# Moving late row loads, reciprocal sums and layer-norm scales of a two-layer attention and gated-MLP kernel to GpSimd

## The chip, the cores and the metric

The kernel runs on one NeuronCore of a Trainium2 chip. The metric is the device time of one execution in microseconds (us). "Before" and "changed" are always timed on the same chip, in the same rounds. In the lines of the profile PE is TensorE (matmuls), PEld its weight loads, DVE is VectorE, ACT is ScalarE, POOL is GpSimd and SP is SyncE, which here only issues transfers. L691 is line 691 of the kernel that is profiled; the same statement has another number in each version.

## The reference

A linear attention layer A and a gated MLP layer B, each behind a layer norm, each applied twice with the same weights, on 2048 rows of 512 numbers in bfloat16:

```python
phi_k = concat([softmax(k @ w_phi), softmax(-(k @ w_phi))])    # 32 heads of 16 features, so sums over 16
kv = einsum("bhsf,bhsd->bhfd", phi_k, v);  z = phi_k.sum(rows)
o  = (phi_q @ kv) / (phi_q @ z + 1e-6)                          # phi_q as phi_k
A(x) = o @ wo
B(x) = (relu(x @ W_gate) * (x @ W_up)) @ W_down
x = x + A(layernorm(x));  x = x + B(layernorm(x));  # and both once more
```

## The kernel before

The program is written as a list of operations with guessed durations (`ii`: how long the engine is held, `lat`: when the result is there). A scheduler walks through them in simulated time, with recorded priorities (`RANKS`), and so fixes the order of instructions on each engine; semaphores are then placed.

The rows are worked on in 16 tiles of 128 rows. For each tile of the first layer: statistics on VectorE, their scale by Ln and Exp on ACT, the normalised tile y on VectorE or GpSimd, its transpose by a DMA from SyncE, key and value matmuls, and then the softmax of the keys:

```python
# ln(l, ts), cut: the scale of one or two tiles
op("act", lambda e: e.activation(lnv[:, a:b, :], mv[:, a:b, 1:2], ACT.Ln, bias=eps[:]), ..., ii=186, lat=295)
op("act", lambda e: e.activation(rstd[:, a:b, :], lnv[:, a:b, :], ACT.Exp, scale=-0.5), ..., ii=94, lat=203)
...
# kv_tile(l, t), cut: exp(+-k), sums over 16 features, their reciprocals, normalised features
for s in range(2):
    op("act", lambda e, s=s: e.activation(ft.ap()[:, s, :], kt.ap(), ACT.Exp, scale=(1.0, -1.0)[s]), ...)
op("dve", lambda e: e.tensor_reduce(zt..., ft..., AX.X, ALU.add), ..., ii=1105, name=f"Z{l}.{t}")
if (l, t) in ACT_RZ:                     # all 16 tiles of the first layer
    op("act", lambda e: e.activation(zt.ap(), zt.ap(), ACT.Ln), ..., ii=150)
    op("act", lambda e: e.activation(rt.ap(), zt.ap(), ACT.Exp, scale=-1.0), ..., ii=150)
else:
    op("dve", lambda e: e.reciprocal(rt.ap(), zt.ap()), ..., ii=420)
op("dve", lambda e: e.tensor_tensor(ft..., ft..., rt... .to_broadcast([P, 32, 16, 2]), ALU.mult), ..., name=f"norm{l}.{t}")
...
# loads: rows 8 to 15 are issued by SyncE, late, between the transposes of y
for t in range(8, 16, 4):
    load_x("sp", t, t + 4)
```

The sums over all tiles of key features times values ("kv sums", L716) need the normalised features of every tile, so TensorE must have VectorE's last tile before the first attention layer can go on.

The softmax here doesn't subtract the row's maximum and nothing guards it: scores larger than these inputs give would overflow.

## Time and profile before

The median was 394.14 us (392.99 to 395.31).

| what | us | view |
|---|---|---|
| span of the profiled run | 392.4 | head of the page |
| TensorE busy | 377.8 (96%) | page, part 1 |
| VectorE, ACT, GpSimd busy | 298.3, 195.4, 42.0 | page, part 1 |
| TensorE waiting for others, all waits of 0.2 us and more | 9.1 (the prediction says 9.5) | waits of TensorE |

Head of the page of the kernel before, and the busy tenths in 40 equal slices of the span (one slice is 9.8 us):

```profile
span 392.4 us, 6587 instructions
...
PE 377.8 (96%) x2413; PEld 212.8 (54%) x2455; DVE 298.3 (76%) x641; ACT 195.4 (50%) x606; POOL 42.0 (11%) x117
...
PE   7889999999999999999999999999999999999996
...
DVE  8799979999897769647678996989998648623424
...
POOL 2006003211211000000000000233102110000000
PEclk9999999999999999999999999999999999999999
```

TensorE is nearly always busy, from the first slice to the last, at a full granted clock. Only a wait of TensorE that goes away can shorten this kernel. This is the table of waits of TensorE in the kernel before: who waited for whom, us in total, times, longest:

```profile
PE pb L586 <- DMA yT<-in_A_wqkv_dram: 1.9, 2, 1.1
PE pb L652 <- DMA yT<-y: 1.7, 2, 1.4
...
PE pb L681 <- DMA wv<-in_A_wqkv_dram: 0.8, 1, 0.8
...
```

The 1.9 us are the transposed loads of the query weights, 1.4 of the 1.7 us a wait for the transposes of y at 24.9 us. The timeline of SyncE's queue (start, duration, engine, line) shows what stands in front of those transposes:

```profile
19.43 0.58 SPq L515 DMA_DIRECT2D x_sb<-in_A_x_dram  x1
20.05 5.50 SPq L634 DMA_TRANSPOSE yT<-y  x3
```

The load of rows 8 to 11 goes out at 19.43 us, the transposes follow. In the chain of waits of the page this transfer is given 4.78 us, where the median of 55 transposes is 2.5 us.

### The profile page before, as it was taken

How to read it: one execution, taken by the hardware profiler on the slowest of the kernel's cores; microseconds unless marked ns; L12 is line 12 of the kernel's file. 1: busy time of each engine (PE TensorE's matmuls, PEld its weight loads, DVE VectorE, ACT ScalarE, POOL GpSimd, SP SyncE). 2: the span in 40 equal slices, each digit the busy share in tenths (PEclk: the TensorE clock that was granted, in tenths of full speed). 3: DMA queues.
4: the chain of work that ended last, by engine and by line, in shares of the span. 5: the costliest groups of instructions: out<-in, count | busy, mean ns of one | idle time of the engine just before them, and what ended most of it. 6: DMA issues, size and time to landing. Idle time of an engine off the chain costs nothing.

```text
span 392.4 us, 6587 instructions
## 1 busy us (share of the span) xinstructions
PE 377.8 (96%) x2413; PEld 212.8 (54%) x2455; DVE 298.3 (76%) x641; ACT 195.4 (50%) x606; POOL 42.0 (11%) x117
## 2 busy tenths in 40 slices
PE   7889999999999999999999999999999999999996
PEld 6434574767655544444444457477865544544443
DVE  8799979999897769647678996989998648623424
ACT  5889969637444235334334574875634333113120
POOL 2006003211211000000000000233102110000000
PEclk9999999999999999999999999999999999999999
DMA  8464492243213221200202000014522221210102
GB/s 217 59 157 70 119 339 81 43 69 67 55 28 80 55 42 27 41 1 13 42 0 42 15 13 2 8 35 69 79 57 55 54 55 40 49 47 0 43 0 67
DMA packets 63008, 22.89 MB, mean 58 GB/s; under 512 B 53920, under 2 KB 62976, under 8 KB 62976
## 3 DMA queue, kind: packets, MB, share of 16 engines
q1 hardware_dynamic: 60144, 20.40, 24.2%
q10 hardware_dynamic: 2832, 2.08, 1.7%
q8 instruction: 19, 0.31, 0.3%
q14 instruction: 13, 0.11, 0.1%
HBM read 7.91 MB, written 2.10 MB: 26 GB/s over the span
## 4 chain that ended last, share of the span: by engine, by line
PE 78%; DVE 10%; DMA 4%; ACT 3%; SPq 2%; issue 1%; POOL 0%
PE pb L842 34%; PE pb L896 17%; PE pb L812 6%; PE pb L681 4%; PE pb L716 4%; PE pb L652 3%; PE pb L749 3%; PE pb L696 3%; PE pb L870 3%; DMA yT<-y 2%; PE pb L898 2%; DVE t L786 2%; DVE z L664 1%; ACT expq L700 1%; DVE stats L600 1%; DMA yT<-in_A_wqkv_dram 1%
## 5 line engine op out<-in xcount | busy, mean ns | idle before, releaser
L850 DVE TENSOR_TENSOR hT<-gate,pb 128x512 bf16<-128x512 bf16 (+1 forms) x100 | 57.4, 576 | 40.6 <-PE pb L842 35.9
L849 ACT ACTIVATE gate<-pb 128x512 bf16<-128x512 f32 (+1 forms) x100 | 50.9, 509 | 69.3 <-PE pb L842 68.7
L842 PE MATMUL pb<-yT,Wu 128*128 128x512 bf16 (+1 forms) x392 | 83.1, 336 | 0.3
L842 PE MATMUL pb<-yT,Wg 128*128 128x512 bf16 (+1 forms) x396 | 81.5, 336 | 0.3
L896 PE MATMUL pb<-Wd,hT 128*128 128x512 bf16 (+2 forms) x322 | 76.0, 372 | 0.3
L842 PEld LDWEIGHTS pb<-yT,Wg 128*128 128x128 bf16 x400 | 38.5, 98 | 29.2 <-DVE x_sb L815 0.2
L842 PEld LDWEIGHTS pb<-yT,Wu 128*128 128x128 bf16 x400 | 38.5, 98 | 28.7
L896 PEld LDWEIGHTS pb<-Wd,hT 128*128 128x128 bf16 x330 | 31.6, 98 | 35.1 <-ACT gate L849 0.3
L664 DVE TENSOR_REDUCE z<-phik 128x64 f32<-128x1024 bf16 x32 | 38.3, 1208 | 8.0 <-ACT phik L663 7.8
L600 DVE BATCH_NORM_STATS2 stats<-x_sb 128x6 f32<-128x512 bf16 x64 | 43.4, 686 | 0.5 <-DMA x_sb<-in_A_x_dram 0.2
L700 ACT ACTIVATE expq<-pb 128x512 bf16<-128x512 f32 x64 | 36.1, 610 | 13.8 <-PE pb L696 13.8
L663 ACT ACTIVATE phik<-pb 128x512 bf16<-128x512 f32 x64 | 35.6, 611 | 11.8 <-PE pb L652 11.8
L786 DVE TENSOR_TENSOR t<-pb,sm 128x384 bf16<-128x384 f32 x64 | 34.1, 550 | 0.8 <-POOL sm L776 0.3
L681 PE MATMUL pb<-wv,yT 128*128 128x512 bf16 x125 | 31.6, 379 | 1.8 <-DMA wv<-in_A_wqkv_dram 0.8
L603 ACT ACTIVATE lnv<-mv,eps 128x1 f32<-128x1 f32 (+1 forms) x58 | 16.9, 298 | 32.6 <-DVE mv L601 32.3
L812 PE MATMUL pb<-wo,oT 128*128 128x512 bf16 x120 | 31.3, 379 | 1.2 <-DMA oT<-o 0.4
L652 PE MATMUL pb<-Wkp,yT 128*128 128x512 bf16 x118 | 30.1, 379 | 2.0 <-DMA yT<-y 1.7
L904 DVE TENSOR_TENSOR x_sb<-x_sb,pb 128x512 bf16<-128x512 bf16 (+2 forms) x33 | 21.9, 665 | 12.8 <-PE pb L898 12.7
L696 PE MATMUL pb<-yT,Wqp 128*128 128x512 bf16 x124 | 31.0, 379 | 0.5 <-DVE t L786 0.3
L620 DVE TENSOR_SCALAR y<-x_sb,mv,rstd 128x512 bf16<-128x512 bf16 x59 | 25.0, 425 | 4.5 <-ACT rstd L605 3.8
L763 ACT ACTIVATE sm<-pb 128x48 f32<-128x48 f32 (+1 forms) x96 | 15.6, 212 | 18.9 <-PE pb L749 18.9
L749 PE MATMUL pb<-kvs,expq 128*128 128x144 bf16 x256 | 23.9, 226 | 0.7 <-ACT expq L700 0.6
(77 smaller groups left out, 384.7 us busy)
## 6 DMA issues: line engine op xcount, KB each, us to landing
out_dram<-x_sb ACTq DMA_DIRECT2D x15, 128.0 KB, 1.7
x_sb<-in_A_x_dram SPq DMA_DIRECT2D x3, 512.0 KB, 4.1
Wg<-in_B_W_gate_dram SPq DMA_DIRECT2D x2, 640.0 KB, 8.0
Wu<-in_B_W_up_dram SPq DMA_DIRECT2D x2, 640.0 KB, 9.0
Wd<-in_B_W_down_dram SPq DMA_DIRECT2D x1, 1280.0 KB, 13.0
yT<-y SPq DMA_TRANSPOSE x55, 2.5
Wd<-in_A_wqkv_dram SPq DMA_DIRECT2D x2, 256.0 KB, 2.9
wv<-in_A_wqkv_dram SPq DMA_DIRECT2D x1, 512.0 KB, 6.5
```

Of the source, the lines that this page charges most:

```text
L600: op("dve", lambda e, t=t: e.bn_stats(stats[:, t, :], x_sb[:, t, :]), reads=[res("x", t)], writes=[res("st", t)], ii=600, lat=690, name=f" ...
L652: i = e.matmul(kt.ap(), src.ap()[:, ic, c0:c0 + 128], Wkp[:, ic, :], start=(ic == 0), stop=(ic == 3))
L664: op("dve", lambda e: e.tensor_reduce(zt.ap().rearrange("p (a b) -> p a b", b=2), ft.ap().rearrange("p s (a f b) -> p (s a) b f", f=16, b= ...
L681: i = e.matmul(vt.ap(), src.ap()[:, ic, c0:c0 + 128], wv[:, ic, :], start=(ic == 0), stop=(ic == 3))
L696: i = e.matmul(qt.ap(), Wqp[:, ic, c * 128:(c + 1) * 128], src.ap()[:, ic, :], start=(ic == 0), stop=(ic == 3))
L700: op("act", lambda e, g=g: e.activation(es[g][0].ap(), qt.ap(), ACT.Exp, scale=(1.0, -1.0)[g]), reads=[qr], writes=[es[g][1]], ii=477, lat ...
L786: return e.tensor_tensor(tt_.ap()[:, b, 0:384].rearrange("p (c h d) -> p c h d", h=8, d=16), pt.ap()[:, 0:432].rearrange("p (c w) -> p c w ...
L812: i = e.matmul(wt.ap(), oT_.ap()[:, c, :], wo[:, c, :], start=(c == 0), stop=(c == 3))
L842: i = e.matmul(pt.ap()[:, 0:n], W[:, ic, fc * 128:(fc + 1) * 128], src.ap()[:, ic, a * 128:b * 128], start=(ic == 0), stop=(ic == 3))
L849: op("act", lambda e: e.activation(st_.ap()[:, 0:n], gt.ap()[:, 0:n], ACT.Relu), reads=[gr], writes=[sr], ii=110 + n * .72, lat=230 + n * ...
L850: op("dve", lambda e: e.tensor_tensor(ht.ap()[:, a * 128:b * 128], st_.ap()[:, 0:n], ut.ap()[:, 0:n], ALU.mult), reads=[sr, ur], writes=[h ...
L896: i = e.matmul(pt.ap()[:, 0:n1 - n0], hT[l, s, fc].ap()[:, c:c + 128], Wd[:, fc, n0:n1], start=(fc == 0), stop=False)
```

## The change

Its intent: ACT and VectorE are nearly full between 20 and 50 us and GpSimd is busy for only 7.1 of these 30 us, so GpSimd gets work. Three parts: rows 8 to 15 are loaded early by GpSimd's own queue; reciprocals of four tiles' sums and six layer-norm scales are computed on GpSimd as powers (z to the -1, variance to the -0.5); the sums of four tiles are halved once on GpSimd before VectorE reduces them. Priorities and choices of engines were searched anew (two long constants, left out).

```diff
+    for k, v in enumerate((-0.5, -1.0)):
+        op("pool", lambda e, k=k, v=v: e.memset(expo[:, k:k + 1], v), ...)
-    for t in range(8, 16, 4):
-        load_x("sp", t, t + 4)
+    for t, k in ((8, c_wv), (12, res("x", 7))):       # after wv, after rows 4 to 7
+        load("pool", lambda e, t=t: e.dma_start(x_sb[:, t:t + 4, :], xv[:, t:t + 4, :]), ..., after=k.writers)
 ...
+        if (l, a) in POW_LN:
+            op("pool", lambda e: e.tensor_tensor(lnv[:, a:b, :], mv[:, a:b, 1:2], eps[:]..., ALU.add), ..., ii=200)
+            op("pool", lambda e: e.tensor_tensor(rstd[:, a:b, :], lnv[:, a:b, :], expo[:, 0:1]..., ALU.pow), ..., ii=300)
+        else:
             # Ln and Exp on ACT as before
 ...
+        if (l, t) in POOL_Z:
+            op("pool", lambda e: e.tensor_tensor(zh..., v()[:, :, 0:8, :], v()[:, :, 8:16, :], ALU.add), ..., ii=1050, name=f"Zp{l}.{t}")
+            op("dve", lambda e: e.tensor_reduce(zt.ap(), zh..., AX.X, ALU.add), ..., ii=590, name=f"Zh{l}.{t}")
+        else:
             # the whole sum on VectorE as before
 ...
+        elif (l, t) in POW_RZ:
+            op("pool", lambda e: e.tensor_tensor(rt.ap(), zt.ap(), expo[:, 1:2].to_broadcast([P, 64]), ALU.pow), ..., ii=700, lat=750, name=f"rZp{l}.{t}")
 ...
-ACT_RZ = {(0, t) for t in range(16)} | {(2, t) for t in range(0, 16, 2)}
+POW_LN = {(0, t) for t in (4, 6, 8, 10, 12, 14)}
+POOL_Z = {(0, t) for t in (4, 6, 8, 10)}
+POW_RZ = {(0, t) for t in (4, 5, 8, 9)}
+ACT_RZ = {(0, t) for t in range(16)} - POW_RZ | {(2, t) for t in range(0, 16, 2)}
```

## The prediction

> **What bounds the kernel now.** TensorE: the page gives it 377.8 of 392.4 us busy (96%) at full granted clock; in the timeline groups of four 128x512 matmuls start every 0.86 us. The table of waits adds up what TensorE loses to others: 9.5 us in all, of which 1.1 us is the start and about 4.6 us falls between 8 and 44 us: 0.8 for wv, 0.8 and 1.1 for the transposed loads of the query weights, 1.4 (at 24.9 us) and 0.3 for the transposes of y, 0.3 for normalised key features. The rest is the head before 8 us (mostly warm-up matmuls) and 3.5 us of drain at the end, which the change leaves.
>
> So the ceiling is low. DVE and ACT are nearly full between 20 and 50 us, but so is TensorE; work taken from them shortens nothing unless it removes one of those waits.
>
> **What changes, costed.**
> - Rows 8 to 15 leave the SyncE queue, where they were issued at 19.4 and 25.6 us between transposes, and are issued by GpSimd once wv and rows 4 to 7 have landed, about 10 us. The transposes behind the 19.4 us load took 4.8 us instead of the median 2.5 us: that is the 1.4 us wait. It should go. Statistics of rows 8 to 11, which waited for their load at 23.5 us, can fill a 1.9 us VectorE gap at 13.7 us. But the 1 MB now travels beside the query-weight transposes. The Trainium skill (DMA: Bandwidth & Descriptors, Rules for kernel authors) says that other issuing engines give no extra bandwidth; only the order can gain. The new program runs another value tile before the query weights are composed, covering part of that.
> - ACT loses 4 Ln/Exp pairs of key sums (0.28+0.27 us each) and 6 of layer norm (0.31+0.23): 5.4 us; it takes on a few copies (about 0.5 us each).
> - VectorE: four 1.2 us key reductions become half as long (estimate 0.65): -2.2 us; one y fewer, -0.4; fewer copies, about -3; but 11 more small attention products, +2.4 later.
> - GpSimd gains four halvings (estimate 1.1 to 1.6 us each, from its 1.16 us 512-wide add), four 64-wide powers (estimate 0.7 to 1.5), twelve tiny operations (about 0.35 each): 11 to 16 us between 15 and 45 us, where it had about 7 us.
> - GpSimd and VectorE can hold each other up: the pair of VectorE normalisations at 35.5 us took 1.7 instead of 1.3 us beside GpSimd's y tiles. I expect the mean normalisation to grow from 0.70 to about 0.8 us, eating part of VectorE's gain.
> - The whole schedule is recomputed: some 3 us of later waits may move either way by 1 us.
>
> **Critical path.** I count -1.4 (y transposes), -1 of the 1.9 us at the query weights, perhaps -0.5 elsewhere, +0.6 returned to DMA collisions and slower GpSimd chains: about -2.3 us.
>
> **Predicted:** 391.8 us, 8 in 10 between 389.0 and 395.0. Faster by over 2%: 0.04; within 2%: 0.93; slower by over 2%: 0.03.
>
> **What would show it.** Right: TensorE waits drop by 2 to 3 us before 44 us, none on y transposes near 25 us; rows 8 to 11 land before 16 us; ACT busy before 60 us falls by some 4 us with hardly any effect on the span; TensorE busy stays near 378. Wrong: query-weight waits grow beyond 2 us; key-sum matmuls wait for normalised features over 1 us.
>
> **What would make it wrong.** Powers or descriptor work on GpSimd far slower than estimated, so that y tiles behind them in order come late; or a poorer order in the second layer pair.

## The result, and the profile after

The changed kernel takes 431.98 us (431.34 to 432.40, 4 runs), the kernel before in the same rounds 394.66 us (392.99 to 395.31, 4 runs). The ratio is 1.095 (95% interval 1.091 to 1.099): slower by 9.5%, where "within 2%" had been given 93%. A ratio here and below is the mean time of one kernel's runs over that of the other's of the same rounds, so it is not quite the ratio of the medians. Both results are correct.

The head and the tenths of the changed kernel's page (one slice is 10.8 us):

```profile
span 430.3 us, 6638 instructions
...
PE 388.0 (90%) x2455; PEld 217.8 (51%) x2455; DVE 297.0 (69%) x643; ACT 196.1 (46%) x593; POOL 95.7 (22%) x132
...
PE   8972923099999999999999999999999999999997
...
DVE  7936442168899998878663898689998784545333
...
POOL 3599868803122110000000000021121001000000
PEclk9995965579999999999999999999999999999999
```

GpSimd is busy 95.7 instead of 42.0 us, with six to nine tenths from the third to the eighth slice where it had had six in the fourth and at most three in the others. TensorE, which had no slice under six tenths, has 2 in the fourth and sixth slice, 3 in the seventh and 0 in the eighth; VectorE, full before, falls to between 1 and 6 tenths; and TensorE's granted clock goes down to half. After the ninth slice (97 us) the rows look as before. GpSimd's groups by form (busy us, mean ns, then its own idle time before) name the work:

```profile
L691 POOL TENSOR_TENSOR rz<-z,expo 128x64 bf16<-128x64 f32 x4 | 43.0, 10762 | 5.6 <-DVE z L680 3.7 <-DVE z L683 1.9
...
L679 POOL TENSOR_TENSOR t<-phik 128x512 f32<-128x512 bf16 x4 | 5.0, 1261 | 1.5 <-ACT phik L674 1.5
...
L611 POOL TENSOR_TENSOR rstd<-lnv,expo 128x2 f32<-128x2 f32 x6 | 4.6, 763 | 0.3
```

Four powers of 128x64 take 43.0 us, 10.76 us each. The group had been guessed at 0.7 us by the kernel's author and at 0.7 to 1.5 us by the prediction. The halvings take 1.26 us, as estimated; the powers of two columns take 0.76 us where "about 0.35" was said. Who waited:

```profile
DVE phik L694 <- POOL rz L691: 38.1, 4, 9.8
```

```profile
PE pb L738 <- DVE phik L694: 16.8, 2, 10.0
PE pb L663 <- DMA yT<-y: 10.0, 1, 10.0
PE pb L703 <- ACT phik L674: 7.6, 1, 7.6
...
PE pb L591 <- DMA yT<-in_A_wqkv_dram: 0.7, 2, 0.5
```

Each of the four normalisations on VectorE waits 8.9 to 9.8 us for its power. VectorE does its instructions in the order that the program fixed (the traces of before, of the changed kernel and of the runs below agree in it), so the sums, normalisations and y tiles behind it stand still as well; other y tiles stand behind the power on GpSimd. Through this TensorE waits three ways: for transposes of y (10.0 us), for a bank that ACT has to empty (7.6), for normalised features (16.8, two waits). None of these names GpSimd: only the chain of waits, followed back, does. In order of time (start, us; the y whose transpose ended the wait of 10.0 us is one of VectorE's, behind the first normalisation that waited):

```profile
24.97 10.61 POOL rz L691
...
35.61 0.04 DVE phik L694
...
36.39 0.30 DVE y L631
...
36.72 3.20 DMA yT<-y
...
46.95 10.94 POOL rz L691
...
61.54 10.53 POOL rz L691
...
74.00 10.91 POOL rz L691
```

The waits that the prediction had counted did shrink in this profile (by how much differs between executions, see below). In the changed kernel TensorE waits 0.7 us for the query weights (1.9 before), and neither the wait for wv (0.8) nor the one for y's transposes at 24.9 us (1.4) is in its table up to 30 us. Of the sum predicted, the sources of gain were there in kind; a term of the cost was off by a factor of seven to fifteen.

### The profile page after: what moved, and what is told of

The parts are those of the page before. It is cut to its first block, busy times and chain, and to the rows that moved or that the text cites. A ratio compares the mean times of both kernels' runs of the same rounds, so it can differ in the third digit from the quotient of the medians.

```text
span 430.3 us, 6638 instructions
## 1 busy us (share of the span) xinstructions
PE 388.0 (90%) x2455; PEld 217.8 (51%) x2455; DVE 297.0 (69%) x643; ACT 196.1 (46%) x593; POOL 95.7 (22%) x132
## 4 chain that ended last, share of the span: by engine, by line
PE 74%; POOL 12%; DVE 6%; DMA 3%; ACT 3%; issue 1%; SPq 1%; POOLq 0%
PE pb L864 31%; PE pb L918 16%; POOL rz L691 10%; PE pb L834 6%; PE pb L703 4%; PE pb L718 4%; PE pb L663 4%; PE pb L738 3%; PE pb L771 3%; PE pb L892 2%; PE pb L920 2%; DMA wv<-in_A_wqkv_dram 2%; DVE stats L605 1%; ACT expq L722 1%; DVE z L683 1%; DVE y L631 1%
## 5 line engine op out<-in xcount | busy, mean ns | idle before, releaser
L864 PE MATMUL pb<-yT,Wg 128*128 128x512 bf16 (+1 forms) x400 | 82.4, 337 | 0.5 <-DVE hr L899 0.5
L694 DVE TENSOR_TENSOR phik<-phik,rz 128x1024 bf16<-128x1024 bf16 x32 | 22.4, 711 | 39.4 <-POOL rz L691 38.1
L691 POOL TENSOR_TENSOR rz<-z,expo 128x64 bf16<-128x64 f32 x4 | 43.0, 10762 | 5.6 <-DVE z L680 3.7
L792 POOL TENSOR_TENSOR sm<-sm 128x64 f32<-128x64 f32 x19 | 6.3, 333 | 157.6 <-ACT sm L785 157.6
L703 PE MATMUL pb<-wv,yT 128*128 128x512 bf16 x128 | 34.1, 403 | 7.7 <-ACT phik L674 7.6
L663 PE MATMUL pb<-Wkp,yT 128*128 128x512 bf16 x124 | 31.9, 387 | 10.0 <-DMA yT<-y 10.0
L722 ACT ACTIVATE expq<-pb 128x512 bf16<-128x512 f32 x64 | 35.4, 610 | 10.4 <-PE pb L718 10.4
L674 ACT ACTIVATE phik<-pb 128x512 bf16<-128x512 f32 x64 | 34.7, 602 | 8.5 <-PE pb L663 8.3
L683 DVE TENSOR_REDUCE z<-phik 128x64 f32<-128x1024 bf16 x28 | 33.5, 1210 | 7.0 <-ACT phik L674 6.9
L738 PE MATMUL pb<-vaug,phik 128*128 128x129 bf16 x256 | 19.8, 247 | 16.8 <-DVE phik L694 16.8
L834 PE MATMUL pb<-wo,oT 128*128 128x512 bf16 x128 | 32.9, 380 | 0.9 <-DMA oT<-o 0.9
```

Of the source, the lines that this page charges most:

```text
L663: i = e.matmul(kt.ap(), src.ap()[:, ic, c0:c0 + 128], Wkp[:, ic, :], start=(ic == 0), stop=(ic == 3))
L683: op("dve", lambda e: e.tensor_reduce(zt.ap().rearrange("p (a b) -> p a b", b=2), ft.ap().rearrange("p s (a f b) -> p (s a) b f", f=16, b= ...
L691: op("pool", lambda e: e.tensor_tensor(rt.ap(), zt.ap(), expo[:, 1:2].to_broadcast([P, 64]), ALU.pow), reads=zr + [c_expo], writes=[rzr], ...
L703: i = e.matmul(vt.ap(), src.ap()[:, ic, c0:c0 + 128], wv[:, ic, :], start=(ic == 0), stop=(ic == 3))
L722: op("act", lambda e, g=g: e.activation(es[g][0].ap(), qt.ap(), ACT.Exp, scale=(1.0, -1.0)[g]), reads=[qr], writes=[es[g][1]], ii=477, lat ...
L834: i = e.matmul(wt.ap(), oT_.ap()[:, c, :], wo[:, c, :], start=(c == 0), stop=(c == 3))
```

## The experiments

Theory A: raising to a power is itself slow on GpSimd, with a cost for every column, and the four wide powers alone make the loss, each one for its full length. Rival B: the instruction is slow because of what surrounds it: the issuing of the loads on GpSimd (two issues, 0.87 us each on average), VectorE at work beside it, the broadcast operand, the bfloat16 output. Rival C: the powers only show a wait that the early loads or the new order make.

To keep the comparison clean the edits below are made after scheduling: an operation gets another engine or function but keeps its place, so the order of all other instructions is that of the kernel it starts from (compared instruction by instruction). The diffs are shortened to the lines that matter, some of them put in words.

### One word: power to addition

```diff
-e.tensor_tensor(rt.ap(), zt.ap(), expo[:, 1:2].to_broadcast([P, 64]), ALU.pow)
+e.tensor_tensor(rt.ap(), zt.ap(), expo[:, 1:2].to_broadcast([P, 64]), ALU.add)
```

Its output is wrong, which doesn't matter for the time.

> The changed program with one word different: the four 64-wide powers on GpSimd become additions with the same operands (wrong result on purpose, every engine's order unchanged). Theory A (raising to a power is itself slow on GpSimd, about 0.17 us per element of the row): each of the four falls from 10.8 us to about 0.33 us, TensorE's 34 us of new waits vanish, total 389 to 394 us. Rival B (the operation is slow because of its surroundings: descriptor work for the loads on GpSimd, [...]the broadcast operand or the bf16 output): the addition stays long, several us each, total above 405 us. Rival C (the powers are only where the wait shows; the early loads or the new order are the cause): total stays above 410 us.

Measured: 391.87 us (391.65 to 392.56), ratio 0.9925 to before (0.989 to 0.996). GpSimd's groups by form:

```profile
L691 POOL TENSOR_TENSOR rz<-z,expo 128x64 bf16<-128x64 f32 x4 | 2.6, 662 | 7.5 <-DVE z L680 4.3 <-DVE z L683 3.2
```

With the same operands, shapes, types, loads and order the instruction takes 0.66 us on average (0.29 to 1.27 us; 0.33 was expected) and all of the loss is gone. Rival B falls, except for a part: something does hold it up by a few tenths to a microsecond. Rival C falls: the loads and the order are unchanged and the time is even below before. The 391.87 us also happen to be the time predicted; this is a program without the wide powers, as the prediction had in effect assumed.

### Powers of 4, 8, 16 and 32 columns

```diff
+WIDTH = {4: 4, 5: 8, 8: 16, 9: 32}
+    i = e.tensor_tensor(rt.ap()[:, 0:w], zt.ap()[:, 0:w], expo[:, 1:2].to_broadcast([P, w]), ALU.pow)
+    i = e.tensor_tensor(rt.ap()[:, w:64], zt.ap()[:, w:64], expo[:, 1:2].to_broadcast([P, 64 - w]), ALU.add)
```

> The changed program with powers on only the first 4, 8, 16 and 32 of the 64 columns of the four tiles and additions on the rest (wrong result on purpose, order unchanged). Theory A: the four powers take about 1.1, 1.8, 3.1 and 5.8 us (0.44 us plus 0.161 us per column, the line through the 2-wide 0.76 us and the 64-wide 10.76 us); GpSimd's power time falls from 43 to about 12 us and the total to some 400 us, between the addition and the full powers. Rival B: times do not follow the width.

Measured: 402.26 us, ratio 1.018 (1.015 to 1.022). The timeline of GpSimd, powers only:

```profile
25.16 1.76 POOL L692 TENSOR_TENSOR rz<-z,expo 128x8 bf16<-128x8 f32 x1
...
38.36 3.29 POOL L692 TENSOR_TENSOR rz<-z,expo 128x16 bf16<-128x16 f32 x1 [0.25 <-DVE z L680]
...
45.53 1.02 POOL L692 TENSOR_TENSOR rz<-z,expo 128x4 bf16<-128x4 f32 x1 [3.65 <-DVE z L680]
...
49.25 5.80 POOL L692 TENSOR_TENSOR rz<-z,expo 128x32 bf16<-128x32 f32 x1 [1.93 <-DVE z L683]
```

| columns | 2 (layer norm) | 4 | 8 | 16 | 32 | 64 |
|---|---|---|---|---|---|---|
| us | 0.70 | 1.02 | 1.76 | 3.29 | 5.80 | 10.76 |

(0.70 is the mean of the six short powers in the run with additions; in the changed kernel it is 0.76.) From 2 to 64 columns the slope is (10.76 - 0.70) / 62 = 0.162 us per column, and the line through these two ends gives 1.0, 1.7, 3.0 and 5.6 us for the four between, against 1.02, 1.76, 3.29 and 5.80 measured. So the cost follows the width, as theory A has it: at 64 columns the part that grows with the width makes 10.4 of the 10.8 us.

### The wide powers taken out again

```diff
 for t in (4, 5, 8, 9):        # after scheduling, at the place of the power
+    lz = op("act", lambda e: e.activation(zt.ap(), zt.ap(), ACT.Ln))
+    o.eng, o.fn = "act", lambda e: e.activation(rt.ap(), zt.ap(), ACT.Exp, scale=-1.0)
```

> The changed program with only the four reciprocal sums back on ACT as an Ln and an Exp, at the same places of the order (correct result). Theory A: everything lost comes back and the rest of the change is worth a little: 389 to 393 us, TensorE waits before 44 us about 1.5 to 2.5 us. Rival C: still above 410 us.

Measured: 392.86 us, ratio 0.995 (0.992 to 0.998), correct. TensorE's waits of this run:

```profile
...
PE pb L663 <- DMA yT<-y: 1.0, 1, 1.0
PE pb L739 <- ACT vaug L467: 0.6, 1, 0.6
PE pb L739 <- DVE phik L695: 0.5, 1, 0.5
PE pb L591 <- DMA yT<-in_A_wqkv_dram: 0.5, 2, 0.3
...
```

The long ones are gone; of their kinds 1.0, 0.6 and 0.5 us are left. Before 44 us TensorE's waits add up to 3.9 us, 2.9 us without the one at the start, where 1.5 to 2.5 us had been expected; the kernel before has 6.1 us there.

### The powers alone, in the kernel before

```diff
 for t in (4, 5, 8, 9):        # kernel before, after scheduling
+    o.fn = lambda e: e.activation(zt.ap(), zt.ap(), ACT.Copy)          # stands for the Ln
+    p.eng, p.fn = "pool", lambda e: e.tensor_tensor(rt.ap(), zt.ap(), expo[:].to_broadcast([P, 64]), ALU.pow)
```

> The kernel before with nothing changed but the four reciprocal sums made by GpSimd powers (the Ln becomes a Copy of the same size so that the order stays; correct result). Theory A: the powers alone are enough: 10.8 us each, total 420 to 436 us. Rival C: total under 405 us.

Measured: 434.08 us, ratio 1.099 (1.094 to 1.104), correct. Its groups and waits:

```profile
L965 POOL TENSOR_TENSOR rz<-z,expo 128x64 bf16<-128x64 f32 x4 | 42.1, 10540 | 9.5 <-ACT z L964 9.5
```

```profile
PE pb L684 <- DMA yT<-y: 19.3, 2, 18.6
PE pb L719 <- DVE phik L675: 15.7, 2, 8.7
...
```

The four powers are enough by themselves, without any early load or new order. Together with the run before it they are necessary and sufficient.

### One power only

```diff
-for t in (4, 5, 8, 9):
+for t in (5, 8, 9):           # back to ACT; tile 4 keeps its power
```

> The changed program with the power kept for one tile only (the first, at 25 us) and the other three sums back on ACT (correct). If each power costs its own length wherever it stands in the order, because later y tiles and normalisations queue behind it: about 10 us over the program with none of them (392.9 us), so 400 to 404 us, with one long TensorE wait. If the scheduled slack hides a single one: under 396 us.

Measured: 403.16 us, ratio 1.022 (1.019 to 1.024). The power of tile 4 came at 42.6 us, not at 25 us: the expectation took it for the first in order, and that is tile 5's. It took 10.53 us, and the total is 10.3 us above the version with none (403.16 - 392.86). In TensorE's timeline:

```profile
56.15 4.03 PE L739 MATMUL pb<-vaug,phik 128*128 128x129 bf16 x44 [8.91 <-ACT vaug L467]
```

The wait is put down to ACT's copy of a value tile. Followed back in the timelines of ACT and VectorE of the same run:

```profile
55.06 0.26 ACT L978 ACTIVATE z<-z 128x64 f32<-128x64 f32 x1 [8.82 <-DVE z L683]
...
55.52 1.55 ACT L467 ACTIVATE vaug<-pb 128x512 bf16<-128x512 f32 x3
```

```profile
53.21 0.69 DVE L695 TENSOR_TENSOR phik<-phik,rz 128x1024 bf16<-128x1024 bf16 x1 [8.92 <-POOL rz L691]
53.82 1.21 DVE L683 TENSOR_REDUCE z<-phik 128x64 f32<-128x1024 bf16 x1
```

The copies stand behind an Ln that waited 8.82 us for a sum on VectorE; the sum (53.82 us) stands behind a normalisation that waited 8.92 us for the power. Four engines in order of their queues, and one slow instruction at the root. The slack of the schedule did not hide this power; the places of the other three were not tried alone.

The steps fit one line. Time of the operation on GpSimd that was added, and time of the kernel that was added:

| comparison | GpSimd, us | total, us |
|---|---|---|
| four powers against four additions, changed kernel | 43.0 - 2.6 = 40.4 | 431.98 - 391.87 = 40.1 |
| narrow powers and their additions against additions | 13.4 - 2.6 = 10.8 | 402.26 - 391.87 = 10.4 |
| one power against Ln and Exp on ACT | 10.5 | 10.3 |
| four powers in the kernel before | 42.1 | 434.08 - 394.98 = 39.1 |

(13.4 is the sum of the four powers, 11.9, and of the four additions behind them, 1.6.) Nearly every microsecond of these powers is a microsecond of the kernel (what TensorE's lowered clock costs, see below, is contained in the totals).

### Reciprocals on VectorE instead

```diff
-o = power on GpSimd
+o.eng, o.fn = "dve", lambda e: e.reciprocal(rt.ap(), zt.ap())
```

> The changed program with the four powers replaced one for one by VectorE reciprocals, order kept (correct). VectorE gets four times about 0.5 us between 22 and 50 us, where it is full; TensorE has about 0.5 to 1.2 us of waits on it there. 391.5 to 393.5 us, within 0.3% of the version with Ln and Exp on ACT (392.9 us).

Measured: 393.21 us, ratio 0.996 (0.994 to 0.998), correct. The four take 0.54 us each. One twentieth of the power's time for the same result, and on the engine that was to be relieved; the total does not tell it from the version on ACT.

### What the other parts are worth

Five runs of 5 rounds each, compared with the version with the sums back on ACT (3 rounds, above). They ran on three chips, so the ratios are to be compared and not the medians.

Early loads alone, in the kernel before:

```diff
+o.eng = "pool";  o.deps = o.deps + [wv or x4];  moved behind GpSimd's first memsets
```

> The kernel before with only rows 8 to 15 loaded early from GpSimd's queue, all other orders kept (correct). If the early loads carry the gain that is left once the powers are gone (about 0.5%): TensorE's 1.4 us wait for y's transposes near 25 us goes, total 0.2 to 0.5% under before. Rival, that the gain is the new order: no change, or worse because the loads run beside the query-weight transposes (their waits, 1.9 us, grow).

The sums back on ACT, and the early loads from SyncE:

```diff
+ops["x8"].eng = ops["x12"].eng = "sp"          # same place in the order
```

> The program with reciprocal sums back on ACT, and rows 8 to 15 loaded by SyncE at the same place of the order instead of by GpSimd (correct). If only the moment of the loads matters: within 0.2% of that program, 0.995 of before. If the GpSimd queue itself gains: 0.3% or more slower than it. If GpSimd's descriptor work cost something: 0.2% or more faster.

No powers at all:

```diff
+the six layer-norm scales: Ln and Exp on ACT in place of add and power on GpSimd
```

> No powers at all: reciprocal sums and the six layer-norm scales back on ACT, same order (correct). The two-column powers cost 0.70 us each on GpSimd against 0.54 us for the Ln and Exp pair on ACT; they sit in the chain from statistics to y. If that chain decides anything, this is 0.1 to 0.4% faster than with the powers; if relief of ACT decides, slower by as much. I expect within 0.2% of the program that keeps them, so 0.993 to 0.997 of before.

No powers and no halving, and the same with the short powers kept:

```diff
+Zp: memset of one column on GpSimd (0.1 us);  Zh: the whole tensor_reduce on VectorE
```

> As the run without powers, and the four key sums whole on VectorE again (a tiny memset stands where the halving was; correct). Only the early loads and the new order are left. VectorE gets 2.2 us more work between 30 and 50 us, where it is full. If halving helps: 0.2 to 0.6% slower than the run without powers; if TensorE covers it: within 0.2%.

> Reciprocal sums back on ACT and the key sums whole on VectorE, but the short powers of layer norm stay on GpSimd (correct). The runs with and without halving differed by 0.1% when no powers were left, so: within 0.3% of 392.9 us. If faster than 392.4 us, it is the best correct version so far.

| what is in it (all correct) | median us | ratio to before | 95% interval |
|---|---|---|---|
| kernel before with early loads | 394.95 | 1.002 | 0.999 to 1.004 |
| changed, wide powers out (3 rounds) | 392.86 | 0.995 | 0.992 to 0.998 |
| the same, loads from SyncE | 392.62 | 0.996 | 0.993 to 0.998 |
| the same, halving out | 392.99 | 0.996 | 0.994 to 0.998 |
| wide and short powers out | 393.81 | 0.998 | 0.996 to 1.001 |
| powers and halving out | 393.34 | 0.998 | 0.995 to 1.000 |

The early loads alone gain nothing. Their part of the mechanism is there: the table of waits of that run has

```profile
PE pb L590 <- DMA yT<-in_A_wqkv_dram: 2.0, 2, 1.2
...
PE pb L656 <- DMA yT<-y: 0.6, 1, 0.6
```

so the wait for y's transposes is down from 1.7 to 0.6 us in all, none of it before 30 us. Between 15 and 32 us the longest transpose takes 2.5 us to land, where it was 4.8 us before: that the late load had lengthened it is thereby shown. That its wait would go at full clock is not shown by this profile: after the waits for the query weights, which still cost 2.0 us, the granted clock fell to 0.70 between 15 and 20 us, and TensorE reached the matmul that had waited until 24.88 us only at 25.09 us. The other five executions had a mean clock of 1.0 and were no faster (394.69 to 395.52 us), and the interval excludes the gain of 0.2 to 0.5% that was expected. Which queue issues them makes no difference (0.996 against 0.995). The halving makes none either. The short powers may be worth 0.2 to 0.4%: without them the ratio is 0.998, where 0.993 to 0.997 had been expected. In the same rounds all six executions without them (393.29 to 394.06 us) were slower than all six that had them and loaded from SyncE (392.26 to 393.01 us); but the intervals of the ratios overlap, so this stays open. So does the source of the half per cent: with powers and halving out only the order searched anew and the early loads are left, and that version (0.995 to 1.000) is not clear of the kernel before. No run has the new order with late loads.

### Is TensorE's lowered clock a part of the loss?

The granted clock is 0.50 from 60 to 90 us of the changed kernel. The last 72 small matmuls of the kv sums stand on the chain and start in it. Dummy matmuls were put in front of them:

```diff
+for k in range(130):
+    e.matmul(pt.ap()[:, 432:512], wm.ap()[:, 0:128], wm.ap()[:, 0:80], start=True, stop=True)
```

> The changed program with all four powers, plus 130 dummy matmuls of 80 columns on TensorE, put before the last group of key-value sums that waits some 10 us for the fourth power; they write columns of a bank that nothing reads. If TensorE's lowered clock after the wait (72 small matmuls in 6.8 us where 3.9 us is usual) is part of the loss: those 72 take about 4 us and the total falls by 2 to 3 us, to 429 to 430 us. If the clock costs nothing on the critical path: no change.

Measured: 432.87 us, ratio 1.097 (1.095 to 1.100), and a wrong result, which was not intended: the dummies write unused columns of a bank in which sums are under way, and it is supposed, not shown, that they disturb those. TensorE's timeline, without and then with the dummies:

```profile
72.93 2.76 PE L738 MATMUL pb<-vaug,phik 128*128 128x129 bf16 x24 [6.86 <-DVE phik L694]
85.68 6.84 PE L738 MATMUL pb<-vaug,phik 128*128 128x129 bf16 x72 [9.98 <-DVE phik L694]
```

```profile
74.12 2.76 PE L739 MATMUL pb<-vaug,phik 128*128 128x129 bf16 x24 [6.87 <-DVE phik L694]
76.67 6.23 PE L982 MATMUL pb<-gate 128*128 128x80 bf16 x130
86.86 5.74 PE L739 MATMUL pb<-vaug,phik 128*128 128x129 bf16 x72 [3.96 <-DVE phik L694]
```

The group got shorter, 5.74 instead of 6.84 us (at a mean granted clock of 0.73 instead of 0.61), not 4 us: the dummies were done 4 us too early. The total did not fall. In this profile all up to there is 1.2 us later, with a wait of 1.1 us for wv at the start, so the group ends at 92.60 instead of 92.52 us, and later waits for the transposes of o are longer (2.6 instead of 0.9 us); the median of the four runs is no lower either. So the lowered clock lengthens this group, which stands on the chain, by at least 1.1 us, but that the total gets shorter without it is not shown, and the size of its share is not settled. An upper end comes from TensorE's busy time: 388.0 us in the changed kernel against 380.1 us with the reciprocals on VectorE, 8 us of 40, of which not all lie on the chain. (The 377.8 us of the kernel before are not the number to compare with: its trace shows 2413 matmuls to 2455 weight loads, so 42 records are missing.)

## Why the prediction was wrong

- **What bounds the kernel: right.** TensorE, 96% busy; only its waits count. With additions in place of the powers TensorE is back at 97%.
- **Gain in the waits: right in kind, its size in part luck.** The waits for wv, the query weights and y's transposes went from 4.1 us to 0.7 us before 30 us in the profile of the changed kernel; in that of the run with dummy matmuls, the same program up to there, they are 2.0 us (1.1 for wv, 0.9 for the query weights), so part of the difference is chance. The version without the wide powers gains 2.1 us on before (394.98 - 392.86; the interval allows 0.8 to 3.4); 2.3 were predicted. But the early loads, which had been given the main part, gain nothing alone, and which part of the change makes the 2.1 us is open.
- **The step that failed: "four 64-wide powers (estimate 0.7 to 1.5)".** They take 10.76 us each, 43.0 us in all. The term "11 to 16 us between 15 and 45 us" for all new work of GpSimd should have been about 54 us (95.7 - 42.0), more than the stage has. The four powers alone were then 43 us on an engine on which y tiles, scales and halvings stand in the same order. In the sum for the critical path their delay was part of "+0.6 returned to DMA collisions and slower GpSimd chains"; the run with additions in place of powers shows that it was 40.1 us. The sign that had been named for this, key-sum matmuls that wait over 1 us for normalised features, is there with 16.8 us.
- **How the estimate came about.** The trace of before has a 64-wide multiplication on GpSimd at 0.33 us and a 512-wide addition at 1.16 us, and no power. The estimate took a power for a somewhat dearer addition, and its lower end equals the 700 ns written in the program, which is a guess of the program and not a measurement. The Trainium skill (GPSIMD Engine Reference, 3.1 Elementwise) puts `tensor_tensor` at about 2.6 cycles per element for an addition. The same page (2.1 Instruction dispatch) says that `tensor_tensor` is a loop in software there; it gives no figure for a power. The trace of the narrow powers agrees that an addition is cheap (0.23 us for 32 columns). That the loop for a power could be another piece of software, with another cost, was the thing to see.
- **"Powers or descriptor work on GpSimd far slower than estimated" stood under what would make it wrong**, with 3% for slower by over 2%. The direction was named and its chance set much too low: for an operation of which no duration had been seen, on an in-order engine that feeds the stage that decides, a factor of ten was a real possibility.
- **Normalisations from 0.70 to "about 0.8" us: wrong and of no weight.** With the wide powers out they take 0.70 us as before; it is the y tiles on VectorE that got longer, 0.66 instead of 0.47 us in the first 60 us; why was not tested.
- **No extra bandwidth from another issuing engine: held.** The Trainium skill (DMA: Bandwidth & Descriptors, Rules for kernel authors) says so, and the traces agree: the two 512 KB loads landed in 6.3 us from GpSimd and in 5.6 us from SyncE (medians), and the kernel's time showed no difference (ratios 0.995 and 0.996).
- **The clock: not foreseen, its share open (at most some 8 of 40 us).** The Trainium skill (TensorE: Matmul & The Clock Gate, Part 1) says that TensorE falls back to half its clock after an idle window of about 3.4 us. The trace agrees: waits of 7 to 10 us, a granted clock of 0.50, and 128x129 matmuls at about 95 ns each (6.84 us for 72, at a mean granted clock of 0.61). The 3.4 us itself no run here shows: in the profile of the early loads alone the clock fell after waits of at most 1.2 us.

No correct version that was run is better than before by more than half a per cent. The best, the changed kernel with its wide reciprocals back on ACT or on VectorE, have ratios of 0.995 and 0.996.

## What to carry to other kernels

Before work is moved to another engine, every operation of the moved work needs a measured duration on that engine at that width; one that no trace shows is measured alone first, and a number written in the program's model does not count. Idle time on an engine says nothing of its speed: the same 64 reciprocals took 0.54 us on VectorE, 0.55 us as two operations on ACT and 10.76 us on GpSimd. And where a wait on the bounding engine names a DMA or another engine, follow the chain back: here three different names stood for one slow instruction.

## What the Trainium skill lacked or had wrong

- GPSIMD Engine Reference, 3.1 Elementwise: of the operations of `tensor_tensor` it tells the cost of an addition only. A power (`tensor_tensor` with `pow`, fp32 in) took 0.162 us per column of 128 partitions on top of some 0.4 us: 1.02, 1.76, 3.29, 5.80 and 10.76 us for 4, 8, 16, 32 and 64 columns, where an addition of 64 columns took from 0.29 us up. At the 1.2 GHz that the page gives (1. Specifications) this is an estimated 194 cycles per column, against its 2.6.
- GPSIMD Engine Reference, 4.1 Engine selection: the table has no row for reciprocals or powers. VectorE's reciprocal of 64 columns took 0.54 us, Ln and Exp on ACT 0.28 and 0.27 us, so a row that sends wide reciprocals to these two and not to GpSimd would help; at 2 columns the power took 0.70 us and the pair on ACT 0.54 us.
